# Transformer block on one core: attention gate per image, fc1 from the second token tile, six accumulator banks, fc1 weights ahead of fc2 weights

## The chip, the cores and the metric

The kernel runs on one core of one Trainium2 chip. The metric is the device time of one execution in microseconds, as the median of several runs. An execution is also recorded once by the hardware profiler; its records are what "the profile" or "the trace" means here. The engines are named as the profile names them: PE is TensorE (matmuls), PEld its weight loads, DVE is VectorE, ACT is ScalarE, POOL is GpSimd, SP is SyncE, which does no arithmetic here and issues most transfers. SPq and POOLq are the transfers issued by SP and by POOL.

## The reference

One block of a diffusion transformer with two images of 256 tokens, width D = 1152, two heads and an inner width of 4608, all in bf16:

```python
mod = (_silu(c) @ w_mod).reshape(B, 6, 1, D)
shift_a, scale_a, gate_a, shift_m, scale_m, gate_m = [mod[:, i] for i in range(6)]
h = _layernorm(x, axis=-1) * (1 + scale_a) + shift_a
qkv = (h @ wqkv).reshape(B, N, 3, H, Dh)
...
attn = _softmax(jnp.einsum('bqhd,bkhd->bhqk', q, k) * Dh ** (-0.5), axis=-1)
a = jnp.einsum('bhqk,bkhd->bqhd', attn, v).reshape(B, N, D) @ wo
x = x + gate_a * a
h2 = _layernorm(x, axis=-1) * (1 + scale_m) + shift_m
m = _gelu(h2 @ w_fc1) @ w_fc2
return x + gate_m * m
```

Six vectors per image come from the conditioning input c. Here `gate_a` ("the attention gate") and `gate_m` ("the mlp gate") matter: the first multiplies the attention's output, the second the output of the two-layer network.

## The kernel before

The 512 tokens are four tiles of 128; tiles 0 and 1 are image 0, tiles 2 and 3 image 1. The program is written once for all engines. Every operation is a unit with an engine, an estimated duration and the memory it reads and writes; a planner (`schedule`) derives the dependencies, keeps TensorE's and SP's units in the order in which they are written, and picks the order of the other engines by priority and by the lists handed to `in_order`. Every engine then works through its own list strictly in order and waits on counters, so an instruction that waits holds up all that stand behind it on its engine. The same is true of the transfers that SP issues (`dma` with the default engine) and of those that POOL issues (`eng="pool"`), which stand in POOL's list between its additions.

The order of the work from the attention on:

- `attn_gate` computes `gate_a` for both images on VectorE while TensorE makes q, k, v and the scores: for each of nine slices of the weights and each image one long step adds weights times a number to `ACCA` (`ga_0_kt` for image 0, `ga_1_kt` for image 1, L1067). Then come, for each image, a transpose (`ga_T0`, `ga_T1`, L1073) and a sum (`ga_red0`, `ga_red1`, L1075), and eight small steps for both images together (`ga_mv1` to `ga_t`, L1079 to L1085). `gate_store` writes the rows to DRAM (`dit_scratch`), and two loads (`ld_g0`, `ld_g1`) bring them back, repeated on all 128 partitions, as `GA[0]` and `GA[1]`. All four transfers stand on SP's list, ahead of the first two blocks of fc1's weights.
- `s_and_softmax` has, for each image and head, a maximum (`smax`), exponentials on ScalarE, a reciprocal (`sri`) and a turn (`PT_turn`, L1025) on VectorE, after which SP issues four small moves.
- `rows` computes scale and shift for the second layer norm on TensorE; VectorE takes them from PSUM banks 3 and 4 (`mt_0`, `mt_1`, L1053). `pv` multiplies probabilities and v; `OT_ev0_7` and `OT_ev1_7` (L700) are VectorE's two copies of its results.
- `wo_tile(t)` multiplies token tile t by `wo` in three pieces of 384 columns, nine matmuls each (`wo_t_c`). VectorE multiplies each piece by the gate of its image (`wo_t1_t_c`, L1171, from PSUM), POOL adds the input (`wo_x1_t_c`, L1172), VectorE takes statistics (L751, L752, L754), POOL makes the scale and offset (L755, L1176, L1177) and ScalarE writes the normalised tile (`xn2_t`, L1178).
- The normalised tile is turned so that its features lie on partitions, and scaled and shifted into `H2T`. Tile 1 is turned on TensorE (`xn2_T(1)`, L706: nine transposes, between the pieces of `wo_tile(3)`), and its nine slices are scaled by VectorE (four, L1194) and ScalarE (five, L1197). Tiles 0, 2 and 3 are turned on VectorE (`h2turn_t`, L1204), moved by four transfers on SP (`mv_h2_t`), and scaled by VectorE (L1217) and ScalarE (L1214).
- `fc1_tile(f, tok0, ntok)` makes 128 of the 4608 inner features for a range of tokens: nine matmuls into one PSUM bank, then one gelu on ScalarE (L1227). The first `F0` features are done for image 0 (tokens 0 to 255) first, of those the first three for each tile of 128 tokens by itself, then for image 1; the rest for all 512 tokens at once. fc1's weights come in nine blocks of four tiles (`wfc1_load`), which share four buffers, so block q waits until the tiles of block q - 4 are done.
- `mlp_gate` computes `gate_m` on VectorE from weights loaded late (`ld_gm`, `WGM`).
- fc2 follows with 13 pieces of 36 matmuls. Its weights come in four loads (`wfc2_load`) of 2.6 MB each.

PSUM has eight banks. `acc_bank` deals them to the wo pieces and the fc1 tiles in turn, from a list `acc` of four, `[3, 4, 5, 2]`; ahead of the second half of fc1 the list is made `[6, 7]` and the four from where they stand, which is `[6, 7, 4, 5, 2, 3]`, and is dealt from its start.

Of the kernel before, what the change touches and what calls it, by code (L numbers as in the profile page):

```python
# [505 lines left out]
P = 128  # L506
# [10 lines left out]
F0 = 14  # L517
# [34 lines left out]
def build_kernel(nc, x, c, wqkv, wo, w_mod, w_fc1, w_fc2, out):  # L552
# [5 lines left out]
    with (  # L558
# [75 lines left out]
        GBA = sb(O_R + FG * 17, 192)[0:32, :]  # L634
        GTA = sb(O_R + FG * 17 + 192, 192)[0:32, :]
# [51 lines left out]
        def dve(cost, fn, reads, writes, name):  # L687
            return S.op("dve", cost, fn, reads=reads, writes=writes, name=name)
# [4 lines left out]
        def pool(cost, fn, reads, writes, name):  # L693
            return S.op("pool", cost, fn, reads=reads, writes=writes, name=name)
# [364 lines left out]
        def attn_gate():  # L1059
# [10 lines left out]
            pool(100, lambda e: e.memset(GBA, 0.0), [], [GBA], "gba0")  # L1070
            for b in range(2):
                a_, t_ = ACCA[:, b, :], ACTA[:, b, :]
                dve(150 + FG * 1.1, lambda e, a_=a_, t_=t_: e.transpose(t_, a_), [a_], [t_], "ga_T%d" % b)  # L1073
                t3, o = t_.rearrange("p (g r) -> p g r", r=32), GPA[:, 0, b, :]
                dve(150 + FG * 1.1, lambda e, t3=t3, o=o: e.tensor_reduce(out=o, in_=t3, axis=AX.X, op=ALU.add), [t3], [o], "ga_red%d" % b)  # L1075
            gp = GPA.rearrange("p q b g -> p q (b g)")
            for q in range(1, 4):
                i_, o_ = gp[32 * q:32 * q + 32, 0, :], gp[0:32, q, :]
                dve(200, lambda e, i_=i_, o_=o_: e.tensor_copy(o_, i_), [i_], [o_], "ga_mv%d" % q)  # L1079
            for a_, b_ in ((0, 1), (2, 3), (0, 2)):  # L1080
                x_, y_ = gp[0:32, a_, :], gp[0:32, b_, :]
                dve(200, lambda e, x_=x_, y_=y_: e.tensor_tensor(out=x_, in0=x_, in1=y_, op=ALU.add), [x_, y_], [x_], "ga_add%d" % b_)
            g0, gb = gp[0:32, 0, :], GBA[:, 0:8 * NG]
            dve(200, lambda e: e.tensor_copy(gb, g0), [g0], [gb], "ga_bf")
            last_red[0] = dve(200, lambda e: e.transpose(GTA, GBA), [GBA], [GTA], "ga_t")  # L1085

        def gate_store():
            lin = scratch[0].rearrange("b (g c) -> (b g) c", c=32)
            dma(lin[0:64].rearrange("(j p) c -> p j c", j=2), GTA[:, 0:64].rearrange("p (j c) -> p j c", j=2), 4096, "st_ga0")
            dma(lin[64:72], GTA[0:8, 64:96], 512, "st_ga1")  # L1090

# [59 lines left out]
        acc = [3, 4, 5, 2]  # L1151
# [123 lines left out]
        wo_tile(3, {2: lambda: xn2_T(1)})  # L1275
# [26 lines left out]
        for t in range(4):  # L1302
# [4 lines left out]
            for (c0, c1) in pieces:  # L1307
# [3 lines left out]
                for j in range(JT):  # L1311
# [8 lines left out]
        ga = ["ga_%d_%d" % (b, kt) for kt in range(KT) for b in range(2)]  # L1320
        S.in_order("dve", ga)
        S.in_order("dve", ga[9:10] + ["smax_0", "snb_0"] + ga[10:11] + ["sri_0"] + ga[11:12] + ["smax_2", "snb_2", "PT_turn0", "smax_1", "snb_1", "sri_2"]
                   + ga[12:13] + ["smax_3", "snb_3", "sri_1", "PT_turn2"] + ga[13:14] + ["PT_turn1", "sri_3"] + ga[14:15] + ["PT_turn3"] + ga[15:16])
# [63 lines left out]
```

## Time and profile before

| | us |
|---|---|
| median of 3 runs | 242.55 |
| the three runs | 242.41 to 242.78 |
| the profiled execution's own time | 244.14 |
| its span, from the first to the last instruction | 242.4 |
| TensorE busy in the span | 235.8 |
| VectorE busy | 121.4 |
| ScalarE busy | 73.2 |
| GpSimd busy | 20.5 |

The granted TensorE clock was 0.993 of full speed on average. In the views below a row of the timeline has the start in us from the start of the span, the length in us, the engine, the line, the operation, what it writes and reads, and how many such instructions were merged; in square brackets stands how long the engine had been idle before it, and what is put down as having ended that idle time. A wait for several things is put down to the one that came last by the profile. A row of the transfers has the size of one and, as its last number, the median time in us from its issue to its landing.

### The profile page before, as it was taken

The page shows a single profiled execution, that of the slowest core. Times are in us where ns is not written, and L with a number is a line of the kernel's source. Part 1 is how long each engine was busy: PE and PEld are TensorE (multiplying, and loading weights), DVE is VectorE, ACT ScalarE, POOL GpSimd, SP SyncE. Part 2 cuts the span into 40 slices and gives each one's busy share as a digit, 9 for nine tenths or more (in the row PEclk, how much of TensorE's full clock was granted, in tenths as well). Part 3 has the DMA queues.
Part 4 walks back from the last instruction along what each step waited for, and adds up shares of the span by engine and source line. Part 5 has one row for each costly group of instructions (what it writes and reads, how often), then busy time and mean ns, then how long its engine had stood idle before and what let it go on. Part 6 is the DMA issues. An engine that isn't in the chain of part 4 may idle for free.

```text
span 242.4 us, 4085 instructions
## 1 busy us (share of the span) xinstructions
PE 235.8 (97%) x1728; PEld 147.6 (61%) x1728; DVE 121.4 (50%) x222; ACT 73.2 (30%) x155; POOL 20.5 (8%) x42
## 2 busy tenths in 40 slices
PE   6899999999999999999998999999999999999995
PEld 2588844456567666887883444444656665665664
DVE  2644469979994598742199997000022222111112
ACT  4922440447635425875332322222000000000000
POOL 1300000000000278310000001200000000000000
PEclk9979999999999999999999999999999999999999
DMA  6999999999590875927999999991000000000000
GB/s 213 366 376 391 389 392 391 395 410 386 168 362 3 230 258 135 308 62 257 388 383 355 388 350 388 368 391 40 0 16 19 16 16 19 16 16 19 20 27 18
DMA packets 34428, 53.00 MB, mean 219 GB/s; under 512 B 4075, under 2 KB 19819, under 8 KB 34411
## 3 DMA queue, kind: packets, MB, share of 16 engines
q1 hardware_dynamic: 34016, 52.14, 61.8%
q0 software_dynamic: 224, 0.59, 0.7%
q8 instruction: 13, 0.21, 0.4%
q10 hardware_dynamic: 171, 0.01, 0.0%
q14 instruction: 4, 0.03, 0.0%
HBM read 50.15 MB, written 1.19 MB: 212 GB/s over the span
## 4 chain that ended last, share of the span: by engine, by line
PE 90%; DVE 3%; DMA 3%; POOL 1%; SPq 1%; issue 1%; ACT 0%; DVEq 0%
PE psum L703 89%; DMA arena<-in_w_mod_dram 3%; DVE arena L1171 1%; SPq L684 1%; DVE arena L751 1%; POOL arena L1172 1%; PE psum L706 0%; DVE arena L1194 0%; DVE arena L1217 0%; ACT arena L1227 0%; POOL arena L755 0%; DVE arena L1315 0%; DVE arena L752 0%; DVE arena L1316 0%; POOL arena L1176 0%
## 5 line engine op out<-in xcount | busy, mean ns | idle before, releaser
L703 PE MATMUL psum<-arena 128*128 128x384 bf16 (+8 forms) x1682 | 233.9, 308 | 3.6 <-POOL arena L729 1.5
L703 PEld LDWEIGHTS psum<-arena 128*128 128x128 bf16 (+1 forms) x1682 | 144.7, 97 | 90.6 <-issue 3.3
L1315 DVE TENSOR_TENSOR arena<-psum,arena 128x384 f32<-128x384 f32 (+2 forms) x13 | 6.9, 528 | 76.1 <-PE psum L703 76.1
L1227 ACT ACTIVATE arena<-psum 128x256 bf16<-128x256 f32 (+2 forms) x53 | 24.0, 460 | 42.2 <-PE psum L703 42.1
L698 ACT ACTIVATE arena<-psum 128x512 bf16<-128x512 f32 (+5 forms) x35 | 18.6, 561 | 31.0 <-PE psum L703 31.0
L1067 DVE SCALAR_TENSOR_TENSOR arena<-arena 128x1152 f32<-128x1152 bf16 x16 | 22.1, 1406 | 0.0
L1100 DVE SCALAR_TENSOR_TENSOR arena<-arena 128x1152 f32<-128x1152 bf16 x16 | 21.3, 1410 | 0.0
L1172 POOL TENSOR_TENSOR arena<-arena 128x384 f32<-128x384 f32 x12 | 10.9, 912 | 71.1 <-DVE arena L1171 71.0
L751 DVE BATCH_NORM_STATS2 arena<-arena 128x6 f32<-128x384 f32 (+1 forms) x18 | 9.7, 551 | 5.6 <-DMA arena<-in_x_dram 4.4
L1178 ACT ACTIVATE arena<-arena 128x1152 bf16<-128x1152 f32 x4 | 5.4, 1348 | 10.2 <-POOL arena L1177 10.2
L1171 DVE TENSOR_TENSOR arena<-psum,arena 128x384 f32<-128x384 f32 x12 | 6.5, 547 | 2.5 <-PE psum L703 2.4
L700 DVE CAST arena<-psum 128x512 bf16<-128x512 f32 x8 | 5.4, 690 | 3.5 <-PE psum L703 3.4
L1316 DVE TENSOR_TENSOR arena<-arena 128x384 bf16<-128x384 f32 (+2 forms) x13 | 6.9, 527 | 0.5
L1204 DVE STREAM_TRANSPOSE arena<-arena 128x1152 bf16<-128x1152 bf16 x3 | 4.1, 1379 | 3.6 <-ACT arena L1178 3.6
L1214 ACT ACTIVATE arena<-arena 128x128 bf16<-128x128 bf16 x12 | 5.0, 482 | 1.0 <-DMA arena<-arena 0.9
L1097 DVE TENSOR_SCALAR arena<-arena 128x1152 f32<-128x1152 bf16 x2 | 1.5, 816 | 7.5 <-DMA arena<-in_w_mod_dram 7.5
L684 POOL DMA_DIRECT2D dit_scratch<-arena x2 | 1.4, 677 | 46.2 <-DVE arena L1115 46.2
L1217 DVE TENSOR_SCALAR arena<-arena 128x128 bf16<-128x128 bf16 x15 | 3.6, 310 | 3.0 <-DMA arena<-arena 3.0
L1018 ACT ACTIVATE arena<-psum,arena 128x256 bf16<-128x256 f32 x8 | 3.7, 469 | 2.4 <-DVE arena L1015 1.9
L706 PEld LDWEIGHTS psum<-arena 128*128 128x128 bf16 (+1 forms) x46 | 3.1, 101 | 1.6 <-DMA arena<-in_c_dram 1.3
L706 PE MATMUL psum<-arena 128*128 128x128 bf16 (+1 forms) x46 | 3.6, 222 | 0.4 <-DMA arena<-in_c_dram 0.4
L755 POOL TENSOR_TENSOR arena<-arena 128x1 f32<-128x1 f32 x6 | 3.4, 564 | 4.3 <-DVE arena L754 4.1
(66 smaller groups left out, 64.6 us busy)
## 6 DMA issues: line engine op xcount, KB each, us to landing
arena<-in_w_fc_dram SPq DMA_DIRECT2D x9, 1152.0 KB, 13.7
arena<-in_w_fc_dram SPq DMA_DIRECT2D x4, 2592.0 KB, 16.8
arena<-in_wqkv_dram SPq DMA_DIRECT2D x18, 288.0 KB, 8.7
arena<-in_w_mod_dram SPq DMA_DIRECT2D x6, 864.0 KB, 12.4
arena<-in_w_mod_dram SPq DMA_DIRECT2D x3, 1728.0 KB, 21.1
arena<-in_wqkv_dram SPq DMA_DIRECT2D x1, 2592.0 KB, 17.9
arena<-in_wo_dram SPq DMA_DIRECT2D x1, 2592.0 KB, 9.6
arena<-in_w_mod_dram SPq DMA_DIRECT2D x1, 2592.0 KB, 10.6
```

The source lines that it names most:

```text
L698: act(c_act(n), lambda e: e.activation(out=dst, in_=src, func=ACTF.Copy), [src], [dst], name)
L700: return dve(c_dve_psum16(n) if psum16 else c_dve_psum32(n), lambda e: e.tensor_copy(dst, src), [src], [dst], name)
L703: S.instr(lambda e: e.matmul(o, lhsT=l, rhs=r, start=st, stop=sp, **kw), reads=[l, r], writes=[o])
L706: S.instr(lambda e: e.transpose(o, i_, idn), reads=[i_, idn], writes=[o])
L751: dve(550, lambda e, s=s, o=o: e.bn_stats(out=o, in_=s), [s], [o], "bn_%s_%d" % (tag, ci))
L1067: ga_units[(b, kt)] = dve(150 + FG * 1.1, lambda e, o=o, w=w, s1=s1: e.scalar_tensor_tensor(out=o, in0=w, scalar=s1, in1=o, op0=ALU.mult, ...
L1100: u = dve(1300, lambda e, o=o, w=w, s1=s1: e.scalar_tensor_tensor(out=o, in0=w, scalar=s1, in1=o, op0=ALU.mult, op1=ALU.add), [w, s1, o], ...
L1171: dve(550, lambda e, o=o, ga=ga, x1c=x1c: e.tensor_tensor(out=x1c, in0=o, in1=ga, op=ALU.mult), [o, ga], [x1c], "wo_t1_%d_%d" % (t, ci))
L1172: S.op("pool", 930, lambda e, xs=xs, x1c=x1c: e.tensor_tensor(out=x1c, in0=x1c, in1=xs, op=ALU.add), reads=[x1c, xs], writes=[x1c], name=" ...
L1227: act(c_act(ntok), lambda e: e.activation(out=dst, in_=o, func=ACTF.Gelu_apprx_tanh), [o], [dst], "gelu_%d_%d" % (f, tok0))
L1315: dve(c_dve_psum32(w), lambda e, o=o, gm=gm, t1=t1: e.tensor_tensor(out=t1, in0=o, in1=gm, op=ALU.mult), [o, gm], [t1], "fc2_t1_%d_%d" % ( ...
L1316: dve(c_dve_32(w), lambda e, t1=t1, x1c=x1c, ost=ost: e.tensor_tensor(out=ost, in0=t1, in1=x1c, op=ALU.add), [t1, x1c], [ost], "fc2_out_%d ...
```

## The change

Seven things change:

1. The attention gate's transpose, sum and small steps are done for image 0 as soon as its nine long steps are done, and those of image 1 after them. The long steps are reordered: the first three slices for both images, then image 0's other six, then image 1's. The small steps are there once for each image (half as wide).
2. Both stores of the gate, and image 0's load, go over POOL's queue; image 1's load stays on SP, behind fc1's first two weight blocks.
3. The bank list is `[2, 3, 4, 6, 5, 7]` from the first wo piece to the end; the change of list between the halves of fc1 is gone.
4. Tile 1's transposes stand one wo piece earlier on TensorE. On VectorE `h2turn_0` comes after tile 1's statistics, and tile 0's three scalings come after the last two wo products; on ScalarE tile 1 is scaled before tile 0.
5. fc1 begins with tile 1's 128 tokens, for five features instead of three, then does the same five for tile 0.
6. `F0` is 15 instead of 14.
7. One of the fc2 loads that stood ahead of fc1's blocks 4 and 5 moves behind them; the three fc2 loads now come ahead of fc1's blocks 6, 7 and 8 in turn.

```diff
-F0 = 14
+F0 = 15
...
-        GBA = sb(O_R + FG * 17, 192)[0:32, :]
-        GTA = sb(O_R + FG * 17 + 192, 192)[0:32, :]
+        GBA = [sb(O_R + FG * 17 + b * 256, 128)[0:32, :] for b in range(2)]
+        GTA = [sb(O_R + FG * 17 + b * 256 + 128, 128)[0:32, :] for b in range(2)]
...
-            gp = GPA.rearrange("p q b g -> p q (b g)")
-            for q in range(1, 4):
-                i_, o_ = gp[32 * q:32 * q + 32, 0, :], gp[0:32, q, :]
-                dve(200, lambda e, i_=i_, o_=o_: e.tensor_copy(o_, i_), [i_], [o_], "ga_mv%d" % q)
...
+                for q in range(1, 4):
+                    i_, o_ = gp[32 * q:32 * q + 32, 0, :], gp[0:32, q, :]
+                    dve(200, lambda e, i_=i_, o_=o_: e.tensor_copy(o_, i_), [i_], [o_], "ga_mv%d_%d" % (b, q))
...
-        def gate_store():
-            lin = scratch[0].rearrange("b (g c) -> (b g) c", c=32)
-            dma(lin[0:64].rearrange("(j p) c -> p j c", j=2), GTA[:, 0:64].rearrange("p (j c) -> p j c", j=2), 4096, "st_ga0")
-            dma(lin[64:72], GTA[0:8, 64:96], 512, "st_ga1")
+        def gate_store(b):
+            lin = scratch[0, b].rearrange("(g c) -> g c", c=32)
+            dma(lin[0:32], GTA[b][:, 0:32], 2048, "st_ga%d_0" % b, eng="pool")
+            dma(lin[32:36], GTA[b][0:4, 32:64], 256, "st_ga%d_1" % b, eng="pool")
+
+        def gate_load(b, eng="sp"):
+            dma(GA[b], scratch[0, b].partition_broadcast(P), P * D * 2, "ld_g%d" % b, eng=eng, run=2304)
...
-        acc = [3, 4, 5, 2]
+        acc = [2, 3, 4, 6, 5, 7]
...
-        gate_store()
-        for b in range(2):
-            dma(GA[b], scratch[0, b].partition_broadcast(P), P * D * 2, "ld_g%d" % b, run=2304)
+        gate_store(0)
+        gate_load(0, "pool")
         wfc1_load(0)
         wfc1_load(1)
+        gate_store(1)
+        gate_load(1)
...
-        wo_tile(3, {2: lambda: xn2_T(1)})
+        wo_tile(3, {1: lambda: xn2_T(1)})
...
-        for tok0 in (0, 128):
-            for f in range(0, 3):
+        for tok0 in (128, 0):
+            for f in range(0, 5):
                 fc1_tile(f, tok0, 128)
-        for f in range(3, F0):
+        for f in range(5, F0):
             fc1_tile(f, 0, 256)
-        wfc2_load(1)
         mlp_gate(last_h2T[0])
-        k = acc_rr[0] % 4
-        acc[:] = [6, 7] + acc[k:] + acc[:k]
-        acc_rr[0] = 0
...
-                if f in (24, 32):
-                    wfc2_load((f - 8) // 8)
+                if f >= 24:
+                    wfc2_load(f // 4 - 5)
                 wfc1_load(f // 4)
...
-        S.in_order("dve", ["ga_t", "mt_0", "mt_1", "OT_ev0_7", "OT_ev1_7"])
...
-                           "bn_ln2_1_0", "wo_t1_1_2", "bn_ln2_1_1", "h2turn_0", "wo_t1_2_0", "bn_ln2_1_2", "aggr_ln2_1", "veps_ln2_1", "wo_t1_2_1", "bn_ln2_2_0", "wo_t1_2_2", "bn_ln2_2_1", "wo_t1_3_0", "bn_ln2_2_2", "aggr_ln2_2", "veps_ln2_2", "h2T_0_0", "h2T_0_3", "h2T_0_6", "wo_t1_3_1",
-                           "h2T_1_0", "h2T_1_1", "h2T_1_2", "h2T_1_3", "bn_ln2_3_0", "wo_t1_3_2", "bn_ln2_3_1", "h2turn_2", "bn_ln2_3_2", "aggr_ln2_3", "veps_ln2_3"])
-        S.in_order("act", ["xn2_0", "xn2_1", "h2T_0_1", "h2T_0_2", "h2T_0_4", "h2T_0_5", "h2T_0_7", "h2T_0_8", "h2T_1_4", "h2T_1_5", "h2T_1_6", "h2T_1_7", "h2T_1_8", "gelu_0_0", "xn2_2"])
+                           "bn_ln2_1_0", "wo_t1_1_2", "bn_ln2_1_1", "wo_t1_2_0", "bn_ln2_1_2", "aggr_ln2_1", "veps_ln2_1", "h2turn_0", "wo_t1_2_1", "bn_ln2_2_0", "wo_t1_2_2", "bn_ln2_2_1",
+                           "wo_t1_3_0", "h2T_1_0", "h2T_1_1", "h2T_1_2", "h2T_1_3", "bn_ln2_2_2", "aggr_ln2_2", "veps_ln2_2", "wo_t1_3_1", "wo_t1_3_2", "h2T_0_0", "h2T_0_3", "h2T_0_6",
+                           "bn_ln2_3_0", "bn_ln2_3_1", "bn_ln2_3_2", "aggr_ln2_3", "veps_ln2_3", "h2turn_2", "h2turn_3"])
+        S.in_order("act", ["xn2_0", "xn2_1", "h2T_1_4", "h2T_1_5", "h2T_1_6", "h2T_1_7", "h2T_1_8", "h2T_0_1", "h2T_0_2", "h2T_0_4", "h2T_0_5", "h2T_0_7", "h2T_0_8", "gelu_0_128", "xn2_2"])
```

The list of VectorE's order in the attention, not shown, now has image 0's transpose, sum and eight small steps between the softmax steps, image 1's remaining six long steps and its transpose, sum and small steps after the last turn of the scores, and then `OT_ev0_7`, `mt_0`, `mt_1`, `OT_ev1_7`. By the planner ScalarE does four gelus of 128 tokens ahead of `xn2_2` and six more ahead of `xn2_3`.

More of the change, by code (lines that the diff above doesn't have):

```diff
@@ new lines, in attn_gate @@
+                for m_, n_ in ((0, 1), (2, 3), (0, 2)):
+                    x_, y_ = gp[0:32, m_, :], gp[0:32, n_, :]
+                    dve(200, lambda e, x_=x_, y_=y_: e.tensor_tensor(out=x_, in0=x_, in1=y_, op=ALU.add), [x_, y_], [x_], "ga_add%d_%d" % (b, n_))
+                g0, gall, gb, gt = gp[0:32, 0, :], GBA[b], GBA[b][:, 0:4 * NG], GTA[b]
+                pool(100, lambda e, gall=gall: e.memset(gall, 0.0), [], [gall], "gba0_%d" % b)
+                dve(200, lambda e, gb=gb, g0=g0: e.tensor_copy(gb, g0), [g0], [gb], "ga_bf%d" % b)
@@ L1319, in build_kernel @@
         S.n_other_dma_sems = 12
[L1320 to L1323, printed above, removed]
+        small = ["ga_%s" % n for n in ("mv%d_1", "mv%d_2", "mv%d_3", "add%d_1", "add%d_3", "add%d_2", "bf%d", "t%d")]
+        S.in_order("dve", ["ga_%d_%d" % (b, kt) for kt in range(3) for b in range(2)] + ["ga_0_%d" % kt for kt in range(3, 7)]
+                   + ["smax_0", "snb_0", "ga_0_7", "sri_0", "ga_0_8", "smax_2", "snb_2", "PT_turn0", "smax_1", "snb_1", "sri_2", "ga_T0",
+                      "smax_3", "snb_3", "sri_1", "PT_turn2", "ga_red0", "PT_turn1", "sri_3"] + [n % 0 for n in small] + ["PT_turn3"]
+                   + ["ga_1_%d" % kt for kt in range(3, KT)] + ["ga_T1", "ga_red1"] + [n % 1 for n in small] + ["OT_ev0_7", "mt_0", "mt_1", "OT_ev1_7"])
         S.in_order("act", ["sexp_0_0", "sexp_0_1", "qk_ev8", "spn_0_0", "spn_0_1", "v_ev0_0", "sexp_2_0", "sexp_2_1", "sexp_1_0", "sexp_1_1", "v_ev0_1",
                            "spn_2_0", "spn_2_1", "spn_1_0", "spn_1_1", "v_ev0_2", "sexp_3_0", "sexp_3_1", "v_ev1_0", "spn_3_0", "spn_3_1", "v_ev1_1", "v_ev1_2"])
-        S.in_order("dve", ["ga_t", "mt_0", "mt_1", "OT_ev0_7", "OT_ev1_7"])
         S.in_order("act", ["OT_ev0_0", "OT_ev0_2", "OT_ev1_0", "OT_ev1_2", "OT_ev_4", "OT_ev0_5", "OT_ev1_5", "gelu_tab", "xn2_0"])
```

12 lines of the change are left out of this document (3 added, 9 removed).

## The prediction, written before the changed kernel had run

> **What bounds the kernel now.** I read the page first, its busy times, then the waits in the timeline.
>
> ```profile
> PE 235.8 (97%) x1728; PEld 147.6 (61%) x1728; DVE 121.4 (50%) x222; ACT 73.2 (30%) x155; POOL 20.5 (8%) x42
> ```
>
> TensorE is busy 235.8 of 242.4 us, and no edit takes a multiplication away. So the change can win only what TensorE loses between matmuls. The two rows of the timeline, cut to its weight loads, that show a wait from 80 us on:
>
> ```profile
> 99.42 30.02 PEld L703 LDWEIGHTS psum<-arena 128*128 128x128 bf16 x270 [0.39 <-DVE arena L1171]
> 130.60 1.42 PEld L703 LDWEIGHTS psum<-arena 128*128 128x128 bf16 x8 [1.17 <-ACT arena L1227]
> ```
>
> Weight loads run ahead of or behind their matmuls, so their idle time sizes a gap only roughly, and a gap spread over many matmuls isn't seen at all. I size the late ones by the gelus (ScalarE, L1227), one behind each fc1 tile, in the timeline:
>
> ```profile
> 110.97 0.38 ACT L1227 ACTIVATE arena<-psum 128x256 bf16<-128x256 f32 x1 [0.60 <-PE psum L703]
> 111.38 1.26 ACT L1214 ACTIVATE arena<-arena 128x128 bf16<-128x128 bf16 x3
> 113.31 0.38 ACT L1227 ACTIVATE arena<-psum 128x256 bf16<-128x256 f32 x1 [0.40 <-PE psum L703]
> 114.30 0.38 ACT L1227 ACTIVATE arena<-psum 128x256 bf16<-128x256 f32 x1 [0.60 <-PE psum L703]
> ...
> 126.09 0.38 ACT L1227 ACTIVATE arena<-psum 128x256 bf16<-128x256 f32 x1 [0.60 <-PE psum L703]
> ...
> 129.97 0.60 ACT L1227 ACTIVATE arena<-psum 128x512 bf16<-128x512 f32 x1 [1.35 <-PE psum L703]
> 132.77 0.60 ACT L1227 ACTIVATE arena<-psum 128x512 bf16<-128x512 f32 x1 [2.21 <-PE psum L703]
> ...
> 148.31 0.60 ACT L1227 ACTIVATE arena<-psum 128x512 bf16<-128x512 f32 x1 [1.34 <-PE psum L703]
> ```
> ```profile
> 111.40 1.43 DVE L1217 TENSOR_SCALAR arena<-arena 128x128 bf16<-128x128 bf16 x6 [2.97 <-DMA arena<-arena]
> ```
>
> Three stalls follow. Stall A, 0.39 us at 99.42: the fourth fc1 tile takes bank 2 of four, which holds the last wo product until VectorE reads it. Stall B: a 256-token tile takes 0.983 us (114.30 to 126.09 in twelve), but from 110.97 two tiles took 113.31 - 110.97 = 2.34 instead of 1.97. That is 0.37 us, spread over single matmuls, each waiting for a slice of tile 3 of h2 that L1214 and L1217 scale only from 111.4. Stall C: a 512-token tile takes 1.943 (132.77 to 148.31 in eight), but 129.97 to 132.77 is 2.80: 0.86 us. The row names a gelu, but tile 16 goes to bank 2 (place 16 mod 6 in [6, 7, 4, 5, 2, 3]), last read after tile 10. The true releaser is the weight block of tiles 16 to 19:
>
> ```profile
> 116.25 0.42 SPq L684 DMA_DIRECT2D arena<-in_w_fc_dram  x1
> arena<-in_w_fc_dram SPq DMA_DIRECT2D x1, 1152.0 KB, 14.2
> ```
>
> 116.25 + 14.2 = 130.45: it landed behind the fc2 block queued ahead of it.
>
> **The change part by part.**
>
> *fc1's blocks ahead of fc2's.* One 2.6 MB fc2 load leaves the place before blocks 4 and 5; no byte is added. Block 4 still waits until tile 3 of the second half has left its buffer (112.4 below + 4 x 0.983 = 116.3), then has only the mlp gate's weights ahead:
>
> ```profile
> arena<-in_w_mod_dram SPq DMA_DIRECT2D x1, 2592.0 KB, 10.6
> ```
> ```profile
> 109.68 0.59 SPq L684 DMA_DIRECT2D arena<-in_w_mod_dram  x1
> ```
>
> Those land at 109.68 + 10.6 = 120.3 at the latest. A block has 1152/2592 of their bytes, below 10.6 x 0.44 = 4.7 us, and is there by 125.0; tile 16 starts at 112.4 + 15 x 0.983 + 1.943 = 129.1. Stall C, -0.86, goes, with 4 us of cover. What is late next: the transfers have the same sum, start no later and meet no gap (block 5 may be issued at 112.4 + 8 x 0.983 = 120.3, while block 4 moves), so the last fc2 block lands no later than now:
>
> ```profile
> arena<-in_w_fc_dram SPq DMA_DIRECT2D x1, 2592.0 KB, 21.1
> ```
> ```profile
> 144.69 6.51 SPq L684 DMA_DIRECT2D arena<-in_w_fc_dram  x1
> ```
>
> That is 144.69 + 21.1 = 165.8. It is wanted after twenty tiles of 1.943 from 129.1, at 168.0. Cover 2.2.
>
> *Six banks, fc1 on tile 1 first.* The steps around it:
>
> ```profile
> 88.45 0.56 DVE L1171 TENSOR_TENSOR arena<-psum,arena 128x384 f32<-128x384 f32 x1 [0.44 <-PE psum L703]
> ...
> 89.53 1.38 DVE L1204 STREAM_TRANSPOSE arena<-arena 128x1152 bf16<-128x1152 bf16 x1
> 90.83 0.52 DVE L1171 TENSOR_TENSOR arena<-psum,arena 128x384 f32<-128x384 f32 x1
> 91.00 2.50 SPq L684 DMA_DIRECT2D arena<-arena  x4
> 91.43 0.91 POOL L1172 TENSOR_TENSOR arena<-arena 128x384 f32<-128x384 f32 x1 [1.43 <-DVE arena L1171]
> 92.12 0.15 DVE L754 TENSOR_SCALAR arena<-arena 128x1 f32<-128x1 f32 x1
> 93.37 1.35 ACT L1178 ACTIVATE arena<-arena 128x1152 bf16<-128x1152 f32 x1 [3.87 <-POOL arena L1177]
> 95.21 2.42 ACT L1214 ACTIVATE arena<-arena 128x128 bf16<-128x128 bf16 x6 [0.49 <-DMA arena<-arena]
> 95.57 0.67 PE L706 MATMUL psum<-arena 128*128 128x128 bf16 x9
> 96.07 3.13 PE L703 MATMUL psum<-arena 128*128 128x384 bf16 x36
> ...
> 104.37 1.34 ACT L1178 ACTIVATE arena<-arena 128x1152 bf16<-128x1152 f32 x1
> ```
> ```profile
> 70.29 0.49 ACT L698 ACTIVATE arena<-psum 128x384 bf16<-128x384 f32 x1 [0.97 <-PE psum L703]
> 71.75 0.49 ACT L698 ACTIVATE arena<-psum 128x384 bf16<-128x384 f32 x1 [0.97 <-PE psum L703]
> ```
>
> A nine-matmul 384 tile takes 1.46 (71.75 - 70.29), nine of 128 columns 0.50 (96.07 - 95.57). The transposes of tile 1 move one tile earlier, to 95.57 - 1.46 = 94.11. They read xn2_1, which now ends at 93.37 + 1.35 = 94.72: alone, the move would cost 0.61. But h2turn_0 (89.53) now stands behind wo_t1_2_0 and tile 1's statistics. VectorE took wo_1_2's product at 88.45, as TensorE ended it, so it can take wo_2_0's (wo_t1_2_0) at 89.91, not 90.83. The chain behind it (L1172 at 91.43, xn2_1 at 93.37) comes 0.92 earlier: xn2_1 ends at 93.80, 0.3 ahead of TensorE. I cost the move at nothing; its bounds are 0 and 0.61.
>
> h2turn_0 then begins when tile 1's variance is done, 92.12 + 0.15 - 0.92 = 91.35, which is 1.82 later. With it slide its four moves (91.00), the wait for them and tile 0's scaling (95.21 + 2.42 = 97.63), now to 99.45. Today's order would stall on that by some 1.5 us, and the other edit covers it: fc1 begins at 96.07 + 1.46 = 97.53 on tile 1 (transposed by 94.8; five scalings of 2.42 / 6 = 0.4 on ScalarE end near 96.8), and five tiles of 0.50 run to 100.04 before tile 0 is asked for. Cover 0.59. The five take banks 2, 3, 4, 6, 5, and the last wo product has bank 7, wanted only at 100.04: stall A, -0.39, goes. Behind tile 0's scaling on ScalarE wait the gelus of the first tiles; bank 2 is wanted again at 100.54, its gelu ends near 99.7.
>
> xn2_2 comes behind four gelus, near 100.2. xn2_3 follows the last 128-token gelu (five more tiles of 0.50 from 100.04, plus its end) near 103.0 instead of 104.37, so tile 3's moves and scaling come some 1.3 earlier, to about 111.5 instead of 111.40 + 1.43 = 112.83. fc1's second half begins at 97.53 + 10 x 0.50 + 10 x 0.983 = 112.4. Stall B, -0.37, goes, with 0.9 of cover; if that cover fails it costs up to 0.37 again.
>
> Two more tiles in halves: 2 x (2 x 0.50 - 0.983) = 0.04. F0 = 15 splits one more 512 tile: 2 x 0.983 - 1.943 = 0.02. Together +0.06.
>
> *Gate per image.* VectorE has 2 x 8 small steps instead of 8:
>
> ```profile
> 62.07 1.39 DVE L1067 SCALAR_TENSOR_TENSOR arena<-arena 128x1152 f32<-128x1152 bf16 x1
> ...
> 63.38 5.14 SPq L684 DMA_DIRECT2D arena<-arena  x8
> ...
> 73.12 0.62 DVE L1079 COPY arena<-arena 32x72 f32<-32x72 f32 x3
> ...
> 74.65 0.27 DVE L1085 STREAM_TRANSPOSE arena<-arena 32x96 bf16<-32x96 bf16 x1
> ...
> 82.34 1.02 DVE L1171 TENSOR_TENSOR arena<-psum,arena 128x384 f32<-128x384 f32 x2 [1.97 <-PE psum L703]
> ```
> ```profile
> 150.49 1.35 POOL L684 DMA_DIRECT2D dit_scratch<-arena  x2 [46.18 <-DVE arena L1115]
> 156.54 1.11 POOL L684 DMA_DIRECT2D arena<-dit_scratch  x2 [4.70 <-DMA dit_scratch<-arena]
> ```
> ```profile
> arena<-dit_scratch SPq DMA_DIRECT2D x2, 288.0 KB, 4.6
> ...
> arena<-dit_scratch POOLq DMA_DIRECT2D x2, 288.0 KB, 7.6
> ```
>
> The eight take 74.92 - 73.12 = 1.8. Image 0's run where a 1.39 step stood (62.07), so its rows are ready at 63.9 and image 1's at 74.92 + 1.8 = 76.7. The mlp gate prices POOL's queue: two stores hold its load back by 156.54 - 150.49 = 6.05, a load lands in 7.6. So image 0 has its gate at 63.9 + 6.05 + 7.6 = 77.6. The first wo product is there at 88.45 - 5 x 1.46 = 81.15 and today waits until 82.34, for the gate. That 1.2 us is worth nothing: by 88.45 VectorE waits 0.44 for TensorE again. Image 1: 76.7 + 6.05 = 82.8, then 4.6 on SP: 87.4; wanted by wo_t1_2_0 at 89.9, so 2.5 of cover. Behind that load on SP stand only tile 0's moves, wanted at 92.74; on POOL nothing before wo_t1_0_0. The scores' last turn follows image 0's steps at 63.9, and SP reaches its four moves only behind four others from 63.38, near 66. Cost: nothing.
>
> No row shows POOL issuing a transfer while VectorE works. Below, the price is 0; above, POOL waits until VectorE is free, at 76.7, which is the first rival. I take 0, since POOL's 0.91 additions run among VectorE's steps (91.43). [...]
>
> **Sum**, against the profiled execution's own 244.14 (span 242.4): -0.39 - 0.37 - 0.86 + 0.06 = -1.56, so 242.58 there. That execution stands 1.59 above the median of 242.55; carried over, 241.0 us.
>
> **The rivals.**
>
> *POOL's queue is late (slower).* POOL writes no descriptors until VectorE rests at 76.7. Stores land at 76.7 + 6.05 = 82.8, image 0's gate at 90.4 instead of 77.6; image 1's stores, behind that load's 0.55 of issue, at 89.4, and its gate at 94.0. wo_2_0 then lacks bank 2. Today xn2_1 ends 12.4 us after wo_t1_0_0 starts (82.34 to 94.72), paced partly by TensorE; that puts it at 102.8, so TensorE stands at most 102.8 - 94.1 = 8.7, and at least 94.0 - 89.9 - 0.3 = 3.8. The middle, 6.2, gives 241.0 + 6.2 = 247.2. It decides once image 1's gate lands 2.8 late (2.5 and 0.3), and is slower than before from 2.8 + 1.56 = 4.4 late on. For it: SP's load took 4.6 where POOL's took 7.6. Against: POOL's prices were taken while SP's queue was full (the 21.1 us load from 144.69).
>
> *One wait takes another's place.* xn2_1 isn't ready at 94.11 (0.3 is thin), up to 0.61 back, or tile 3 is late again, up to 0.37. Both: 242.0; one: 241.5.
>
> *It doesn't do what it says.* Each of the three waits comes back at another place and only the +0.06 is left: 242.6. For it: bytes and VectorE's work keep their sums. Against: the covers of 4, 2.2, 0.9 and 0.59.
>
> **How the numbers follow.** Forecast 0.61, at 240.7 (each stall 0.1 larger than sized) to 241.4 (one unseen wait of 0.4); a new small wait 0.16; nothing won 0.07; POOL late 0.16. 0.2% is 0.49 us, about what a measurement can tell from none. Faster 0.77, within 0.07, slower 0.16. Range: below to 240.6, since the forecast's low side has 0.1 of scatter on it; above to 243.0, which takes in both small waits, nothing won and the start of the POOL case.
>
> **What would show it.** Right: no wait of TensorE at fc1's start, before the second half or at tile 16; fc1's 512 tiles from 127.1; transposes of tile 1 at 94.1. Wrong: POOL's first store landing after 75, a wait of L706 for L1178, the step wo_t1_2_0 released by a transfer.

## The result, and the profile after

| us | before | after |
|---|---|---|
| median | 242.66 (4 runs) | 241.06 (4 runs) |
| lowest to highest | 242.41 to 242.78 | 240.89 to 241.41 |
| profiled execution, and its span | 244.14, 242.4 | 241.23, 239.3 |
| span from `rows` to the end | 167.55 | 166.00 |

After is to before as 0.9943, with a 95% interval of 0.9931 to 0.9955: 1.60 us less by the medians.

The two profiled executions differ by 3.1 us in span, twice as much as the medians. The page's row of the granted clock shows why, of before and then of after:

```profile
PEclk9979999999999999999999999999999999999999
```
```profile
PEclk9999999999999999999999999999999999999999
```

Before's third slice has 7 tenths. In the timeline, cut to TensorE, the same sixteen multiplications stand there, of before and of after:

```profile
11.36 3.52 PE L703 MATMUL psum<-arena 128*128 128x256 bf16 x16 [0.38 <-DVE arena L830]
```
```profile
10.88 1.91 PE L703 MATMUL psum<-arena 128*128 128x256 bf16 x16 [0.37 <-DVE arena L830]
```

They took 1.6 us longer, at half clock (0.50 from 11.47 to 14.88 us), in a part that the change doesn't touch; two of the runs below, which have most of the change, show the same 7 in their third slice, and the same mean granted clock of 0.993. So that profiles can be compared, every time below counts from the first weight load of the stage `rows`, which is the row of 72 loads in the timeline of weight loads. Of after:

```profile
73.25 2.06 PEld L703 LDWEIGHTS psum<-arena 128*2 128x2 bf16 x72 [0.21 <-issue]
...
92.34 0.65 PEld L706 LDWEIGHTS psum<-arena 128*128 128x128 bf16 x9
92.94 143.68 PEld L703 LDWEIGHTS psum<-arena 128*128 128x128 bf16 x990
```

Before has that row at 74.85, so a time of the prediction stands 1.60 earlier in after's views. From there to the end is "the stretch": 242.4 - 74.85 = 167.55 before, 166.00 after (the span without rounding is 239.25). 1.55 less: the whole gain lies there. It is read from one execution each; the waits found below add up to the differences between stretches to 0.03, in one run to 0.1.

The last two rows are the result: from 92.34 on the weight loads run to the end in one piece. The breaks of before at 99.42 and 130.60 are gone, and the waits of TensorE, as a view of their own, are those of the kernel's start:

```profile
PE psum L703 <- POOL arena L729: 1.5, 1, 1.5
PE psum L706 <- DMA arena<-in_c_dram: 0.4, 1, 0.4
PE psum L703 <- DVE arena L830: 0.4, 1, 0.4
PE psum L703 <- DMA arena<-in_w_mod_dram: 0.3, 1, 0.3
PE psum L703 <- issue: 0.2, 1, 0.2
```

Before has 0.7 for L1227 and 0.2 for L1171 there. The slow tiles ahead of fc1's second half (stall B) show in the gelus, which have line L1229 now:

```profile
111.96 0.38 ACT L1229 ACTIVATE arena<-psum 128x256 bf16<-128x256 f32 x1 [0.60 <-PE psum L703]
112.94 0.38 ACT L1229 ACTIVATE arena<-psum 128x256 bf16<-128x256 f32 x1 [0.60 <-PE psum L703]
...
127.65 0.60 ACT L1229 ACTIVATE arena<-psum 128x512 bf16<-128x512 f32 x1 [1.56 <-PE psum L703]
129.60 0.60 ACT L1229 ACTIVATE arena<-psum 128x512 bf16<-128x512 f32 x1 [1.35 <-PE psum L703]
```

From 111.96 each tile takes 0.98, and tile 16 follows tile 15 after 129.60 - 127.65 = 1.95 where before had 2.80.

Where no row sizes a stall below, it is the time between the starts of two successive matmuls in the trace less what one takes. By that measure after has no gap over 0.01 us from 76.3 to the end, and before had 0.39 (stall A), 0.38 (stall B, in three waits of some 0.11 and a few smaller ones) and 0.86 (stall C).

### The profile page after: what moved, and what is told of

Same layout as the page of the kernel before. It is cut to its first block, busy times and chain, and to the rows that moved or that the text cites. A ratio compares the mean times of both kernels' runs of the same rounds, so it can differ in the third digit from the quotient of the medians.

```text
span 239.3 us, 4153 instructions
## 1 busy us (share of the span) xinstructions
PE 234.0 (98%) x1752; PEld 148.2 (62%) x1755; DVE 124.4 (52%) x230; ACT 73.2 (31%) x158; POOL 23.5 (10%) x48
## 3 DMA queue, kind: packets, MB, share of 16 engines
HBM read 50.15 MB, written 1.19 MB: 215 GB/s over the span
## 4 chain that ended last, share of the span: by engine, by line
PE 91%; DMA 5%; SPq 3%; issue 0%; DVE 0%
PE psum L703 90%; DMA arena<-in_w_mod_dram 5%; SPq L684 3%; PE psum L706 0%; DVE arena L1314 0%; DVE arena L1315 0%
## 5 line engine op out<-in xcount | busy, mean ns | idle before, releaser
L1229 ACT ACTIVATE arena<-psum 128x256 bf16<-128x256 f32 (+2 forms) x56 | 23.8, 442 | 39.3 <-PE psum L703 39.3
L1067 DVE SCALAR_TENSOR_TENSOR arena<-arena 128x1152 f32<-128x1152 bf16 x16 | 22.5, 1411 | 0.2
L684 POOL DMA_DIRECT2D dit_scratch<-arena x6 | 3.5, 583 | 101.4 <-DVE arena L1084 53.9
L700 DVE CAST arena<-psum 128x512 bf16<-128x512 f32 x8 | 5.4, 684 | 4.5 <-PE psum L703 4.5
L1219 DVE TENSOR_SCALAR arena<-arena 128x128 bf16<-128x128 bf16 x15 | 4.7, 379 | 3.8 <-DMA arena<-arena 3.8
```

Of the source, the lines that this page charges most:

```text
L684: return S.op(eng, 500.0 if eng == "sp" else 150.0, lambda e: e.dma_start(dst, src), reads=[src], writes=[dst], name=name, dma_bytes=nbyte ...
L1067: ga_units[(b, kt)] = dve(150 + FG * 1.1, lambda e, o=o, w=w, s1=s1: e.scalar_tensor_tensor(out=o, in0=w, scalar=s1, in1=o, op0=ALU.mult, ...
L1229: act(c_act(ntok), lambda e: e.activation(out=dst, in_=o, func=ACTF.Gelu_apprx_tanh), [o], [dst], "gelu_%d_%d" % (f, tok0))
```

## The experiments

Each run is compared by its stretch. Four kernels were timed often enough for a ratio to the kernel before on the same chip, whose median was 242.83 beside the first three of them and 242.63 beside the last.

| run | stretch expected | measured |
|---|---|---|
| weight order alone | 166.7 | 166.70 |
| old weight order | 167.2, rival 166.9 | 166.96 |
| old gate | 166.0 | 165.98 |
| turn of tile 0 early | 166.6 | 166.70 |
| image 1's gate late | 168.0 to 168.2 | 170.07 |
| the same, wait filled | 168.4, rival 170.0 | 168.17 |
| transposes at the old place | 166.3 to 166.6 | 166.93 |
| four banks | 166.0 to 166.2, rival from 166.4 | 166.79 |
| tile 0 first | 167.3 to 167.6 | 168.34 |
| three split features | 165.94, rival 166.4 to 166.7 | 166.68 |
| three, new order | 165.94, rival over 166.1 | 165.99 |
| copies beside the stores | 166.00 | 166.45 |

### The order of the weights, alone and taken back

The kernel before with nothing but the new order of the weights:

```diff
-        wfc2_load(1)
         mlp_gate(last_h2T[0])
...
-                if f in (24, 32):
-                    wfc2_load((f - 8) // 8)
+                if f >= 24:
+                    wfc2_load(f // 4 - 5)
```

> The kernel before, with only the order of the fc1 and fc2 weight loads changed. The yardstick is the stretch from the first weight load of the rows stage to the end of the span, which leaves the start of the kernel out: 167.55 us before (242.40 - 74.85), 166.00 in the changed kernel (239.25 - 73.25). Theory of three stalls (A 0.39 at fc1's start, B 0.37 before fc1's second half, C 0.86 at tile 16): C alone goes, so 166.7, and the time falls by 0.86 from 242.6 to about 241.8; waits of 0.39 at fc1's start stay. Rival, that the late weights only move: another block is late and the stretch stays at 167.4 to 167.6.

Measured: 241.87 (8 runs), ratio 0.9961 (0.9933 to 0.9988). Its weight loads:

```profile
94.45 3.01 PEld L703 LDWEIGHTS psum<-arena 128*128 128x128 bf16 x36
97.86 139.52 PEld L703 LDWEIGHTS psum<-arena 128*128 128x128 bf16 x918 [0.40 <-DVE arena L1171]
```

Stall A is there (97.86), the break at tile 16 is not. The stretch fell by 0.85, the size of stall C.

The changed kernel with those lines as they were:

> The changed kernel with the old order of the weight loads. Three stalls: C comes back, and larger than it was, since block 4's landing hangs on the mlp gate's weights (10.2 us behind their landing before) and TensorE is there 1 us sooner: landing at 118.5 + 10.2 = 128.7, tile 16 wanted at 127.5, so a wait of 1.2 and a stretch of 167.2; time about 242.3. Rival, C is a fixed 0.86: 166.9. Rival, the order did nothing: 166.0.

Measured: 242.03 (10 runs), ratio 0.9973 (0.9952 to 0.9994). One stall is left, of 0.96:

```profile
128.01 109.19 PEld L703 LDWEIGHTS psum<-arena 128*128 128x128 bf16 x648 [1.26 <-ACT arena L1229]
```
```profile
PE psum L703 <- DMA arena<-in_w_fc_dram: 0.8, 1, 0.8
```

So the view of the waits names the weights, where the timeline's row names a gelu. The rows of block 4's transfer, whose last number is the time from issue to landing, say the same, of this kernel and of the changed one:

```profile
arena<-in_w_fc_dram SPq DMA_DIRECT2D x1, 1152.0 KB, 13.4
```
```profile
arena<-in_w_fc_dram SPq DMA_DIRECT2D x1, 1152.0 KB, 6.8
```

Issued at 114.53 it landed at 127.9 with the old order; issued at 114.90, at 121.7 with the new. Tile 16 wants it at about 128.01 - 0.96 = 127.1. Alone the order brings 0.85, and without it 0.96 of the gain is lost. It is rather more without it because, counted from `rows`, TensorE is at tile 16 some 0.71 earlier than in the kernel before, and the block lands only 0.62 earlier (127.90 - 72.87 = 55.03, where before has 130.50 - 74.85 = 55.65). The expected 1.2 had the block landing 0.4 later than it did.

### The gate per image

The changed kernel with the gate computed, stored and loaded as before, all on SP, and with VectorE's old order up to `OT_ev1_7`. The part of the edit that moves the transfers:

```diff
-        gate_store(0)
-        gate_load(0, "pool")
+        gate_store()
+        for b in range(2):
+            dma(GA[b], scratch[0, b].partition_broadcast(P), P * D * 2, "ld_g%d" % b, run=2304)
         wfc1_load(0)
         wfc1_load(1)
-        gate_store(1)
-        gate_load(1)
```

> The changed kernel with the attention gate as before: both images together, all four transfers on SP. Three stalls: the gate per image is worth nothing, so the stretch is 166.0 within 0.1 and the time that of the changed kernel (0.994 of before), although the first wo product waits for its gate until some 1.2 us after TensorE has it. Rival, the earlier gate is part of the gain: up to 1.2 us slower, 166.5 to 167.2.

Measured: 241.11 (4 runs), ratio 0.9922 (0.9893 to 0.995). The gate per image is worth nothing here, as costed.

What a late gate would cost: image 1's load is made to wait for `wo_t1_1_2`.

```diff
-        gate_load(1)
+        late = gate_load(1)
...
+        late.instrs[0].deps.add([u for u in S.units if u.name == "wo_t1_1_2"][0].instrs[0])
```

> The changed kernel with one wait added: SP's load of image 1's gate also waits for the step wo_t1_1_2. The gate then lands near 87.4 + 3.2 = 90.6 where it landed at 84.0, and wo_t1_2_0 wants it at 88.3. The prediction's cover: what is late beyond the wanted time, 2.3, less 0.1 to 0.3, comes back on TensorE at tile 1's transposes: stretch 168.0 to 168.2 instead of 166.0. Rival, six banks and later slack take it up: 166.0 to 166.5.

Measured: 245.53 in its one run. The timeline of the two stations of the wait, then of the weight loads behind it:

```profile
91.14 0.56 DVE L1173 TENSOR_TENSOR arena<-psum,arena 128x384 f32<-128x384 f32 x1 [2.94 <-PE psum L703]
...
95.12 1.14 PE L706 MATMUL psum<-arena 128*128 128x128 bf16 x9 [2.24 <-ACT arena L1180]
```
```profile
96.38 0.15 PEld L703 LDWEIGHTS psum<-arena 128*128 128x128 bf16 x1 [0.17 <-issue]
96.70 0.15 PEld L703 LDWEIGHTS psum<-arena 128*128 128x128 bf16 x1 [0.17 <-issue]
...
98.30 141.77 PEld L703 LDWEIGHTS psum<-arena 128*128 128x128 bf16 x959 [0.17 <-issue]
```

The load was issued at 87.65, and the late gate came out as a wait of the transposes for xn2_1, as the slower rival has it: `wo_t1_2_0`, at 91.14, stands at 88.31 in the changed kernel. But the stretch grew by 4.07, and the wait is 2.41. Behind it nine transposes take 1.14 instead of 0.67, and the loads of the next wo piece start 0.32 apart instead of 1.46 / 9 = 0.16: for 3.41 us, to 98.5, TensorE ran at half speed, which is the other 1.65.

To tell the idle time from the moment, the same kernel does the first wo piece of tile 3 twice, so that 1.46 of the wait is work:

```diff
-                for g in range(KT):
+                for g in [g for _ in range(2 if (t, ci) == (3, 0) else 1) for g in range(KT)]:
```

> Image 1's gate late as in the run where its load waits for wo_t1_1_2 (stretch 170.07: a wait of 2.41 and then 3.41 us at half clock), but TensorE does the first wo piece of tile 3 twice, so that 1.46 of the 2.41 us are matmuls whose result is written over. Theory: the half clock is the answer to the idle time itself. Then the wait is 0.95, no matmul takes double time, and the stretch is 166.00 + 2.41 = 168.4. Rival: the half clock comes at that time whatever TensorE does (a window that runs by itself, or the power of the moment): the stretch is again 170.0 or so. The result is the reference's either way.

Measured: a wait of 0.69 and no matmul of double time behind it.

```profile
94.80 0.68 PE L706 MATMUL psum<-arena 128*128 128x128 bf16 x9 [0.52 <-ACT arena L1180]
```

166.00 + 1.46 + 0.69 = 168.15 is the stretch (168.17). With 1.46 us more work the kernel is 1.90 us faster, and the mean granted clock of the execution is 1.0, where it was 0.993 with the wait unfilled: the half clock came with the wait of 2.41 and not with that of 0.69, by one execution of each kernel. What makes it come is not found by that. The granted clock of the traces changes in steps of 3.41 us (in the kernel before to 0.50 at 11.47 and back to 1.00 at 14.88). Of the run with the late gate, the step ahead of the half clock and the half clock itself, with the busy time of PE, PEld, DVE, ACT and POOL in each, and then the clock:

```profile
91.69:95.10 3.41, 1.19 (x8) 0.49 (x5) 3.34 (x8) 1.35 (x1) 2.50 (x5) 1.00 0.00 0
95.10:98.51 3.41, 3.39 (x17) 2.15 (x18) 3.06 (x10) 2.14 (x6) 2.34 (x5) 0.50 0.50 117
```

In the step ahead TensorE is busy for 1.19 us. In the kernel with tile 0 first, below, a step with 1.82 (96.44 to 99.85) is followed by full clock, but at the start of the kernel before a step with 2.36 (8.06 to 11.47), many of whose matmuls have two columns, is followed by half. So busy time alone does not decide it.

The prediction's open question, whether GpSimd can issue transfers while VectorE works, was put to another kind of VectorE step too, copies. Four float32 copies, whose results nothing reads, stand behind image 0's last gate step:

```diff
+                for i in range(4 if b == 0 else 0):
+                    c0, c1 = ACTA[:, 0, :], ACCA[:, 0, :]
+                    dve(800, lambda e, c0=c0, c1=c1: e.tensor_copy(c0, c1), [c1], [c0], "cp_%d" % i)
```

> The changed kernel with four float32 copies of 128x1152 on VectorE (results not used) right behind image 0's last gate step, where GpSimd issues image 0's stores and load. [...] Rival: GpSimd's issuing takes no notice, landing after 5.7 and 5.2 us as before, and the gate lands near 75.2.

The timeline of after, VectorE's row and GpSimd's, and then the same of this kernel:

```profile
62.62 8.63 DVE L1067 SCALAR_TENSOR_TENSOR arena<-arena 128x1152 f32<-128x1152 bf16 x6
```
```profile
62.40 1.26 POOL L684 DMA_DIRECT2D dit_scratch<-arena  x2 [47.41 <-DVE arena L1084]
68.89 0.58 POOL L684 DMA_DIRECT2D arena<-dit_scratch  x1 [5.22 <-DMA dit_scratch<-arena]
```
```profile
62.27 3.09 DVE L1087 COPY arena<-arena 128x1152 f32<-128x1152 f32 x4
```
```profile
62.64 2.02 POOL L684 DMA_DIRECT2D dit_scratch<-arena  x2 [47.10 <-DVE arena L1084]
70.11 0.57 POOL L684 DMA_DIRECT2D arena<-dit_scratch  x1 [5.45 <-DMA dit_scratch<-arena]
```

Under the long steps of L1067 the stores' issue takes 1.26, as in all nine other runs that have these stores and no copies (1.26 to 1.27); under the copies 2.02. The load is issued 6.49 after the stores began, and 7.47 with the copies. So beside the copies GpSimd's issuing took 0.76 longer in this run, and not the 2.6 to 3.1 us that they last. One copy takes 3.09 / 4 = 0.77, so the stores may have waited for single copies; the trace doesn't tell.

The gate itself comes later by more: the load lands at 78.21, 8.1 after its issue where the changed kernel has 6.3. With the 0.23 by which this profile reaches `rows` later taken off, that is 2.8 later than 75.16. The author's estimate was 2 to 3, from the length of the copies (some 2.6); that the issue is held up for so long was not shown. The 2.8 came by another path: 0.98 of it is the later issue, and 1.8 the longer landing, which begins at 70.11, when the copies are long over (65.36). No run shows its cause.

In the changed kernel no copies of that length stand there, and its gates land in time. The stretch grew by 0.45 for another reason: VectorE is 3.09 later with what follows, and TensorE waits at 79.61 for L700 (`OT_ev0_7`, 78.91 to 79.55), whose result the eighth matmul of the first wo piece reads. VectorE's slack up to that step is thus 3.09 - 0.45 = 2.6 us.

### The order around tile 1, and the banks

`h2turn_0` back ahead of `wo_t1_2_0`:

```diff
-"bn_ln2_1_1", "wo_t1_2_0", "bn_ln2_1_2", "aggr_ln2_1", "veps_ln2_1", "h2turn_0",
+"bn_ln2_1_1", "h2turn_0", "wo_t1_2_0", "bn_ln2_1_2", "aggr_ln2_1", "veps_ln2_1",
```

> The changed kernel with h2turn_0 back in its old place on VectorE, ahead of wo_t1_2_0. The prediction's step: xn2_1 then comes 0.92 later, and tile 1's transposes, which now stand one wo piece earlier, wait 0.6 for it: stretch 166.6, with a wait of L706 put down to the normalised tile. Rival, the transposes have slack and h2turn_0's place doesn't matter: 166.0.

Measured: 242.15 in one run, stretch 0.70 longer, in one stall of 0.68 in front of the transposes:

```profile
93.37 0.51 PEld L706 LDWEIGHTS psum<-arena 128*128 128x128 bf16 x9 [0.90 <-ACT arena L1180]
```

The transposes can stand one piece earlier only because that 1.4 us step left xn2_1's chain; the prediction's upper bound for the move alone was 0.61.

Tile 1's transposes back in their place, the rest changed:

```diff
-        wo_tile(3, {1: lambda: xn2_T(1)})
+        wo_tile(3, {2: lambda: xn2_T(1)})
```

> The changed kernel with tile 1's transposes back in their old place, ahead of the last wo piece. Prediction's calendar: tile 1's slices on ScalarE end 1.46 later, after the start of fc1, and tile 0's scaling and the gelus slide behind them: 0.3 to 0.6 lost in small waits at fc1's start, stretch 166.3 to 166.6. Rival, the place of the transposes doesn't matter: 166.0.

fc1 on tile 0 first, with five features each:

```diff
-        for tok0 in (128, 0):
+        for tok0 in (0, 128):
...
-"h2T_0_8", "gelu_0_128", "xn2_2"
+"h2T_0_8", "gelu_0_0", "xn2_2"
```

> The changed kernel with fc1 beginning on tile 0. Prediction: tile 0's last slice is ready 1.5 us after it would be wanted, so 1.3 to 1.6 of waits at fc1's start, and stretch 167.3 to 167.6. Rival, the order of the two tiles matters no more with six banks: 166.0 to 166.3.

Measured: 0.93 and 2.34 longer in one run each, both more than expected, and in both TensorE waits for L1219, tile 0's slices on VectorE (0.5 and 1.8 us in the views of the waits). The first has 0.2 more at 97.99, where fc1's first tile waits for tile 1's slices on ScalarE, the wait that was expected. Of the first kernel the slices and GpSimd's additions beside them, of the second the slices:

```profile
98.96 2.08 DVE L1219 TENSOR_SCALAR arena<-arena 128x128 bf16<-128x128 bf16 x3
```
```profile
98.98 1.78 POOL L1174 TENSOR_TENSOR arena<-arena 128x384 f32<-128x384 f32 x2
```
```profile
96.71 1.82 DVE L1219 TENSOR_SCALAR arena<-arena 128x128 bf16<-128x128 bf16 x3
```

Both orders are needed, tile 1 first above all. The expectations had the three slices at 0.8 us, which they take in the kernel before (L1217 at 96.21); here they take 1.8 and more. That is followed up below.

The old list of four banks for everything:

```diff
-        acc = [2, 3, 4, 6, 5, 7]
+        acc = [3, 4, 5, 2]
```

> The changed kernel with four accumulator banks, 3, 4, 5, 2, from the first wo piece to the end. If stall A is cured by the new order on VectorE and by tile 1 first, only the fifth fc1 tile waits, for the gelu of the first, by about 0.15: stretch 166.0 to 166.2. Rival, the six banks are what cures stall A: 0.39 or more comes back, 166.4 or more.

Measured: 242.3 in one run, stretch 0.79 longer, in two stalls:

```profile
78.60 1.41 PEld L703 LDWEIGHTS psum<-arena 128*128 128x128 bf16 x10 [0.58 <-DVE arena L1053]
...
98.97 138.70 PEld L703 LDWEIGHTS psum<-arena 128*128 128x128 bf16 x936 [0.30 <-ACT arena L1229]
```

The second (0.29) is the price of four banks: the fifth fc1 tile waits for the first one's gelu. The first (0.47) belongs to this list's start: the first wo piece takes bank 3, out of which `mt_0` comes only behind `OT_ev0_7` in the changed order. The run shows that this list of four costs the change about half of its gain. It doesn't show how much of the 0.47 a list of four with another start would keep, nor whether five banks would do.

### Tile 0's slices and GpSimd's additions

Three split features instead of five, with `F0` at 14:

```diff
-F0 = 15
+F0 = 14
...
-            for f in range(0, 5):
+            for f in range(0, 3):
...
-        for f in range(5, F0):
+        for f in range(3, F0):
```

> The changed kernel with three features in 128-token tiles instead of five, and F0 = 14 again. Two theories. (1) Splitting is pure cost and the sixfold bank list and the order carry the change: from the second norm's row stage to the end 165.94 us, 0.06 less than with the change (166.00), no wait of TensorE. (2) The five tiles were needed because tile 0's slices on VectorE are slow while GpSimd adds (0.6 us each, three ending at 98.44): TensorE now asks for tile 0 at 97.43, so its first tile 0 product waits for L1219 and the stretch is 166.4 to 166.7.

The same, with the slices where GpSimd has only its small steps:

```diff
-"wo_t1_3_1", "wo_t1_3_2", "h2T_0_0", "h2T_0_3", "h2T_0_6",
+"h2T_0_0", "h2T_0_3", "h2T_0_6", "wo_t1_3_1", "wo_t1_3_2",
```

> As the one before it (three features, F0 = 14), with tile 0's three slices on VectorE placed ahead of wo_t1_3_1, where GpSimd runs only its small steps of 128x1 and no long addition. If the 0.6 us of a slice in the changed kernel comes from GpSimd's additions beside it, the three take about 0.8 us together, end near 96.3, and no wait is left: stretch 165.94, 0.06 less than with the change. If a slice takes 0.6 us for another reason (its place behind the wo products, its tile), the three still take 1.8 us and the stretch stays above 166.1.

Measured: a stall of 0.66 in the first (99.82), and next to none in the second. Of the first, VectorE's slices (GpSimd's additions run from 97.93) and the matmuls that wait for them; of the second, ScalarE's slices of tile 0 and VectorE's, with the wo products behind them:

```profile
98.16 1.83 DVE L1219 TENSOR_SCALAR arena<-arena 128x128 bf16<-128x128 bf16 x3
```
```profile
99.82 2.44 PE L703 MATMUL psum<-arena 128*128 128x128 bf16 x32 [0.50 <-DVE arena L1219]
```
```profile
95.64 2.42 ACT L1216 ACTIVATE arena<-arena 128x128 bf16<-128x128 bf16 x6 [0.38 <-DMA arena<-arena]
```
```profile
95.73 0.76 DVE L1219 TENSOR_SCALAR arena<-arena 128x128 bf16<-128x128 bf16 x3
96.40 1.02 DVE L1173 TENSOR_TENSOR arena<-psum,arena 128x384 f32<-128x384 f32 x2
```

The same three slices, grouped by line with the shortest, middle and longest duration in ns, in after and in the last kernel:

```profile
L1219 DVE TENSOR_SCALAR arena<-arena x3: 300/745/954, 96.6 to 98.1; 128x128 bf16<-128x128 bf16 x3
```
```profile
L1219 DVE TENSOR_SCALAR arena<-arena x3: 308/309/314, 95.7 to 96.2; 128x128 bf16<-128x128 bf16 x3
```

A slice takes 0.31 us without a long addition of GpSimd beside it, and up to 0.95 with one, while the additions keep their 0.92. Of after's three slices, the two long ones begin while an addition is under way and end 0.05 after it (97.34 and 98.22; the additions end at 97.29 and 98.17), and the third, with next to none beside it, takes 0.30. Tile 1's slices (L1196), which VectorE reads from PSUM, keep their 0.33 beside such an addition (93.74 to 94.07, the addition from 93.65 to 94.56).

The reordered kernel took 241.38 (7 runs, 240.91 to 241.74), ratio 0.9933 (0.9905 to 0.9961), no different from the change's 0.9943. It saves the 0.06 of splitting and pays 0.04 in two small gaps from 98.1 on, where ScalarE's last slice of tile 0 ends at 95.64 + 2.42 = 98.06. So the five split features pay for the slow slices; with another order three do as well.

## Why the prediction was right

The forecast was 1.56 less and 241.0 us; measured were 1.60 less and 241.06. The three waits are gone where it said, the transposes of tile 1 start at 92.50 and fc1's 512 tiles at 125.51, which are 94.10 and 127.11 on its scale. Its terms, by the runs:

- **Stall C, -0.86, and the weights.** Right in size: alone the new order brings 0.85. Block 4 landed 6.8 after its issue at 114.90, so at 121.7, where the forecast had 125.0 - 1.6 = 123.4 at the latest. The last fc2 block landed at 164.5, against 164.2 by the forecast's "no later than now" (165.8 - 1.6): 0.3 off, out of 2.2.
- **Stall A, -0.39.** Right in size: the bank list and the new order around tile 1 together remove it. How much of it each removes stays open, since the runs that take one back bring other waits: with four banks the fifth tile waits 0.29 for a gelu, and with tile 0 first TensorE waits for tile 0's slices.
- **The move of the transposes, nothing.** Right, cover included: xn2_1 ends at 90.89 + 1.35 = 92.24 and the transposes start at 92.50, the 0.3 foreseen. Without the move of `h2turn_0` it costs 0.70.
- **Stall B, -0.37.** Right in size, but the cover was not. Of the 0.9 only 0.1 is left by the same count, from the last slice to the first matmul: tile 3 is scaled by 109.27 + 1.43 = 110.70 and wanted at 112.4 - 1.6 = 110.8. That it was enough is luck. The step that failed is "so tile 3's moves and scaling come some 1.3 earlier". xn2_3 does come 1.45 earlier, and tile 3 is turned by 104.07. But tile 2's moves start 0.7 later than before on this scale, SP issues the eight moves of tiles 2 and 3 back to back, so that tile 3's begin at 104.95, and they end only some 0.5 earlier:

```profile
101.60 5.89 SPq L684 DMA_DIRECT2D arena<-arena  x8
```
```profile
109.27 1.43 DVE L1219 TENSOR_SCALAR arena<-arena 128x128 bf16<-128x128 bf16 x6 [1.24 <-DMA arena<-arena]
```

  (101.60 + 5.89 = 107.49 here; before they end at 109.68, which is 108.1 on this scale, where the mlp gate's load follows them.) The next thing to be late here is SP's issue.
- **The cover of tile 0, 0.59.** Counted from ScalarE's slices alone. Those are done at 95.44 + 2.42 = 97.86 (forecast 99.45 - 1.6), and tile 0 is asked for at 98.43. VectorE's three end at 98.44, since two of them take 0.75 and 0.95 beside GpSimd's additions, which the forecast hadn't in its sum. That it costs nothing is luck: the last of them is for the seventh matmul of nine, 6 x 0.056 = 0.33 later. With three tiles ahead instead of five it cost 0.73.
- **Splits, +0.06.** The three waits as measured, less the splits, give 0.39 + 0.38 + 0.86 - 0.06 = 1.57, where the stretch fell by 1.55.
- **The gate.** Right at nothing. Image 0's load was issued at 68.89, 6.49 after the stores (forecast 6.05), and landed in 6.3 (7.6), at 75.2; the first product is taken at 79.53. Image 1's load landed 3.2 after its issue at 80.83, at 84.0, wanted at 88.31: 4.3 of cover, where the forecast had 2.5, since it had used 4.6 for a load on SP.
- **The slower rival.** GpSimd's stores did not wait for VectorE's 8.63 us (they were issued in 1.26 under them), so it did not come about; its condition failed in the step "POOL writes no descriptors until VectorE rests". Its price for a late gate was a bound on the wait alone. The wait is where the rival put it, but 2.41 of it cost 4.07.
- **1.59 above the median.** The profiled execution of before stood above its median by the half clock in its first 15 us (1.6), which has nothing to do with the change: the kernels with the transposes at the old place and with three split features have it in their profiles too. Carrying the difference over was right.

## What to carry to other kernels

Read a stall from what is late, not from the name that the row gives: the break named after a gelu was a weight block, behind a larger load that nobody needed yet, and moving that load was worth more than half of the gain. When a transfer, a bank and an order each take one small wait away, count the cover of each on every engine that feeds it: here a slice on VectorE, eight issues on SP and the order of one 1.4 us step stood within about 0.3 us of giving part of the gain back. A part that is hidden is worth nothing even when it works (the gate per image), and can be left out.

## What the runs showed of the hardware

- With image 1's gate late, a wait of TensorE of 2.41 us in the middle of the kernel was followed by 3.41 us at half clock (0.50), which cost 1.65 more. Waits of 0.69 (the same, filled), 0.96 (old weight order) and 1.47 (tile 0 first) were not. So this wait was dearer than itself, and filling it with work that nobody needs was cheaper than the wait (168.17 against 170.07, one execution each).
- The half clock of 3.41 us at the kernel's start came in some executions and not in others. Sixteen multiplications took 3.52 us under it and 1.91 without. Of 17 executions of the kernel before on one chip, the two with a mean granted clock of 0.993 took 244.09 and 244.18, where the median is 242.83. In the profile of before no wait between 5.2 us and that half clock is longer than 0.60, so what brings it on stays open.
- A bf16 scaling of 128x128 on VectorE within SBUF took 0.31 us with no long addition of GpSimd beside it (tile 0's slices with three split features and the new order). In the changed kernel the two that began while a float32 addition on GpSimd was under way took 0.75 and 0.95 and ended 0.05 after the addition, which kept its 0.92. Read from PSUM, tile 1's slices took 0.33 beside an addition, four of them 1.09; with the transposes at the old place, where GpSimd was idle, four took 1.10.
- GpSimd issued image 0's two stores in 1.26 us under VectorE's long multiply-adds (the changed kernel) and in 2.02 us under float32 copies (one run).
